# Splitting the row maxima ahead of their transpose in an attention and Fourier-mixing kernel

## The chip, the cores and the metric

The kernel runs on one core of one Trainium2 chip. Its metric is the device time of one execution in microseconds (us). A core has TensorE (PE in the profile; PEld are its weight loads), VectorE (DVE), ScalarE (ACT), GpSimd (POOL) and SyncE (SP), which here only issues DMAs. Each engine takes its instructions in the order in which the program issues them and waits for others through semaphores.

## The reference, cut to what matters

```python
# x: 2048 x 640; 32 heads of 20 columns
g = sigmoid((x * gate_w).sum(-1, keepdims=True))
qkv = (x @ wqkv).reshape(B, S, 3, H, Dh)            # q, k, v per head
scores = einsum("bhqd,bhkd->bhqk", q, k) * Dh ** -0.5
a = einsum("bhqk,bhkd->bhqd", softmax(scores), v)   # -> heads joined, @ wo
b = dft_seq_re @ (x @ dft_hid_re.T) - dft_seq_im @ (x @ dft_hid_im.T)
out = g * a + (1 - g) * b
```

The weights `wqkv` and `wo` are drawn 64 times larger than usual, so scores are large and the softmax needs each row's maximum subtracted before the exponential.

## The kernel before

All is float32. Most matmuls run on numbers rounded to the type fp32r (`R` in the code), each operand split in two rounded parts (`split`: a rounded copy, then the source minus that copy), and three products are added (`three`).

Attention is done by units: a pair of heads and half of the queries (1024), so 32 units (`NU`). Per unit the scores are computed twice. The first time ("m" steps, `s_mm`, line 187) they lie with queries on partitions, and DVE takes the maximum over each 512 keys (line 189) into `mx`. The second time ("e" steps, line 907) they lie with keys on partitions, and ACT takes the exponential (line 909). The negative maximum of each query has to be in the second product already: the query operand `q` has two more rows per head (from row `KROWS`, 60), which hold the two rounded parts of the negative maximum, against rows of ones in the key operand. These rows are filled once per unit:

- `max_nm` (lines 201 to 203): DVE reduces `mx` over the key chunks to `nm`, 128 queries by 16 columns (2 heads, 8 query tiles), negated.
- `max_chain` (lines 218 to 235): TensorE transposes `nm` to 16x128 in a PSUM bank `pt` (line 221; weights are `nm`, the moving operand is the identity), DVE splits it into `m1` and `m2` (lines 114 and 115 through `split`), and two steps later four DMAs on SP's queue copy them to the rows of `q` (lines 229 and 230).

After a first part (projections of q, k, v, the gate), the main part is one loop over 256 cycles. A string of letters in `ORDERS` says in which order TensorE's work is issued in a cycle: "e" and "m" score matmuls, "F" fillers (matmuls of the Fourier part, lines 363 and 608, and of the output projection, line 715), and at the end "B", `burst`:

```python
def burst(c):
    for n in ends:
        max_nm(n)
    run_extras(max(done - HIDS, 0) // 3, 2)
    for kt in (2 * c, 2 * c + 1):
        av_step(now[0], kt // NS, kt % NS)
    while ends:
        max_chain(ends.pop(0))
```

So in every eighth cycle DVE gets `nm` ahead of the 16 matmuls of probabilities by values ("av", line 528), which run in four column tiles of the array, and TensorE gets the transpose behind them. `run_extras` issues the reading of finished Fourier tiles between the two; one of its operations is DVE's addition of line 628. The first unit ends before the loop, where `s_end` calls `max_nm` and, two score steps later, `max_chain`.

The score matmuls and the fillers run in two row tiles of the array (60, 62 or 64 rows). The matmuls of the first part (lines 118 to 120) use the whole array. Five PSUM banks (`bank`) go round among score tiles, transposes and others.

POOL adds and splits the operands of the Fourier part (lines 114, 115, 501, 517, 742). All of its work is from SBUF to SBUF, in instructions of 0.45 to 2.4 us. DVE's work on the maxima reads PSUM, with the exception of `nm`, which reads `mx`.

Of the kernel before, what the change touches and what calls it, by code (L numbers as in the profile page):

```python
# [10 lines left out]
F32 = mybir.dt.float32  # L11
R = mybir.dt.float32r
AF = mybir.ActivationFunctionType
ALU = mybir.AluOpType
AX = mybir.AxisListType
# [3 lines left out]
P = 128  # L19
# [9 lines left out]
KROWS = 3 * DH  # L29
# [41 lines left out]
def f32(ap):  # L71
    return ap.bitcast(F32)
# [3 lines left out]
def mix_kernel(ctx: ExitStack, tc: tile.TileContext, xa, wqk, wb, cdft, wo, out):  # L76
    nc = tc.nc
    pe, act, dve, pool, sp = nc.tensor, nc.scalar, nc.vector, nc.gpsimd, nc.sync
    ctx.enter_context(tc.manual_schedule())

    def pools(**kw):
        return ctx.enter_context(tc.tile_pool(**kw))

    const = pools(name="const", bufs=1)
    small = pools(name="small", bufs=1)
# [14 lines left out]
    ident = const.tile([P, P], F32, name="ident")  # L100
# [9 lines left out]
    def split(dst1, dst2, src, e1, e2):  # L110
        if e1 is act:
            act.activation(dst1, src, AF.Copy)  # L112
        else:
            e1.tensor_copy(dst1, src)  # L114
        e2.tensor_tensor(dst2, src, f32(dst1), op=ALU.subtract)  # L115
# [8 lines left out]
    def bank():  # L124
        return ps_w.tile([P, 512], F32, name=f"ps{next(turn) % 5}")
# [40 lines left out]
    def q_unit(n):  # L166
        p, u = VISITS[n]
        return third["q"] if p == 14 else qst[place(p)][:, u * (S // 2) : (u + 1) * (S // 2)]

    mx, nms, ends = {}, {}, []  # L170
    now, later = [-1], {}

    def at_step(i, fn):
        later.setdefault(i, []).append(fn)
# [16 lines left out]
    def s_end(i):  # L191
        n, s = divmod(i, 32)
        if n < NU and s == 31:
            if now[0] < 0:
                max_nm(n)
            else:
                ends.append(n)
        if s == 1 and 0 < n <= NU and now[0] < 0:
            max_chain(n - 1)

    def max_nm(n):
        nms[n] = small.tile([P, 16], F32, name="nm", bufs=2)
        dve.tensor_reduce(nms[n], mx.pop(n).rearrange("p h q c -> p (h q) c"), axis=AX.X, op=ALU.max, negate=True)

    def s_step(i):
        for fn in [s_mm(i, h) for h in range(2)]:
# [10 lines left out]

    def max_chain(n):
        q = q_unit(n)
        pt = bank()[:16, :P]  # L220
        pe.transpose(pt, nms.pop(n), ident)  # L221
        m1 = small.tile([16, P], R, name="m1")
        m2 = small.tile([16, P], R, name="m2")
        split(m1, m2, pt, dve, dve)

        def rows():
            for h in range(2):
                b = 64 * h + KROWS
                sp.dma_start(f32(q[b : b + 1, :]), f32(m1[8 * h : 8 * h + 8, :]))
                sp.dma_start(f32(q[b + 1 : b + 2, :]), f32(m2[8 * h : 8 * h + 8, :]))  # L230

        if now[0] < 0:
            rows()
        else:
            at_step(now[0] + 2, rows)
# [555 lines left out]
    start = 4 * HID  # L791
# [121 lines left out]
# [8 lines that stand above are left out]
        if c in (HID - NS - 1, HID - 1):  # L921
            next_pool()
# [127 lines left out]
```

## Time and profile before

| | |
|---|---|
| median of 3 runs | 1869.67 us (1867.93 to 1871.03) |
| profiled execution | 1869.47 us |
| its span, first to last instruction | 1867.7 us |
| mean granted TensorE clock | 0.998 |
| DVE `nm`, line 203 | 32 instructions, 210 ns each |
| transpose, line 221: weight load, matmul | 32 each, 87 ns and 277 ns |
| DVE split of `pt`, lines 114 and 115 | 32 each, 278 ns each |

How to read the lines: a timeline line gives the start in us, the duration in us, engine, line, operation, the tile written, an arrow, the tiles read, the shape and a count (instructions merged), and in brackets how long the engine was idle before and what ended that. A line of groups gives the count, busy us and mean ns, and the idle us before. A line of stretches gives the stretch, its length, busy us (and instructions) of PE, PEld, DVE, ACT and POOL, the granted clock, the DMA share and GB/s. The line of a source gives the shortest, median and longest duration in ns. The slices of the page give the busy tenths of an engine in 40 equal parts of the span. Matmul durations include the way through the array, so distances between starts tell more than durations.

### The profile page before, as it was taken

The page shows a single profiled execution, that of the slowest core. Times are in us where ns is not written, and L with a number is a line of the kernel's source. Part 1 is how long each engine was busy: PE and PEld are TensorE (multiplying, and loading weights), DVE is VectorE, ACT ScalarE, POOL GpSimd, SP SyncE. Part 2 cuts the span into 40 slices and gives each one's busy share as a digit, 9 for nine tenths or more (in the row PEclk, how much of TensorE's full clock was granted, in tenths as well). Part 3 has the DMA queues.
Part 4 walks back from the last instruction along what each step waited for, and adds up shares of the span by engine and source line. Part 5 has one row for each costly group of instructions (what it writes and reads, how often), then busy time and mean ns, then how long its engine had stood idle before and what let it go on. Part 6 is the DMA issues. An engine that isn't in the chain of part 4 may idle for free.

```text
span 1867.7 us, 45004 instructions
## 1 busy us (share of the span) xinstructions
PE 1858.3 (100%) x17606; PEld 1360.8 (73%) x17606; DVE 1383.7 (74%) x2310; ACT 1272.1 (68%) x2439; POOL 1162.6 (62%) x1038
## 2 busy tenths in 40 slices
PE   9999999999999999999999999999999999999998
PEld 8988777676767777777777777767777777776666
DVE  3044458787878888888888888888888888888853
ACT  4222258787877777777777777777777777778885
POOL 3335432121146897466799899867779989635544
PEclk9999999999999999999999999999999999999999
DMA  6744341222134674535567576546476766431233
GB/s 230 174 136 151 139 127 56 78 65 68 54 99 139 209 209 142 161 128 175 185 192 241 163 249 191 176 140 179 145 240 203 214 198 202 142 90 47 88 98 108
DMA packets 178771, 281.61 MB, mean 151 GB/s; under 512 B 44811, under 2 KB 113547, under 8 KB 178559
## 3 DMA queue, kind: packets, MB, share of 16 engines
q1 hardware_dynamic: 177599, 276.77, 47.4%
q0 software_dynamic: 960, 1.97, 0.6%
q8 instruction: 138, 2.26, 0.5%
q14 instruction: 74, 0.61, 0.1%
HBM read 214.61 MB, written 63.52 MB: 149 GB/s over the span
## 4 chain that ended last, share of the span: by engine, by line
PE 98%; DMA 1%; POOL 0%; ACT 0%; DVE 0%; issue 0%; SPq 0%; POOLq 0%; ACTq 0%
PE av L528 25%; PE yp L608 19%; PE ps L907 16%; PE ps L187 15%; PE yp L363 7%; PE ps L118 4%; PE ps L120 4%; PE ps L119 4%; PE yp L715 3%; PE ps L221 0%; DMA p<-in_xa 0%; POOL p L115 0%; DMA a_scr<-raw 0%; DVE mx L189 0%; ACT p L323 0%
## 5 line engine op out<-in xcount | busy, mean ns | idle before, releaser
L189 DVE TENSOR_REDUCE mx<-ps 128x1 f32<-128x512 f32 x2048 | 1280.1, 684 | 298.9 <-PE ps L187 280.7
L909 ACT ACTIVATE p<-ps 128x512 f32<-128x512 f32 x2048 | 1109.1, 599 | 371.6 <-PE ps L187 248.9
L187 PE MATMUL ps<-kst,qst 60*128 60x512 f32 x1920 | 758.3, 410 | 0.0
L907 PE MATMUL ps<-qst,kst 62*128 62x512 f32 x1920 | 744.9, 407 | 0.1
L608 PE MATMUL yp<-x,part 64*128 64x320 f32 x5376 | 662.1, 306 | 0.3 <-ACT raw L373 0.3
L608 PEld LDWEIGHTS yp<-x,part 64*128 64x128 f32 x5376 | 624.7, 186 | 8.3 <-ACT raw L373 0.6
L528 PE MATMUL av<-p,v 128*21 128x512 f32 x4096 | 490.1, 596 | 0.0
L907 PEld LDWEIGHTS ps<-qst,kst 62*128 62x128 f32 x1920 | 348.1, 185 | 182.5 <-DVE mx L189 132.2
L187 PEld LDWEIGHTS ps<-kst,qst 60*128 60x128 f32 x1920 | 342.2, 184 | 7.9 <-issue 4.2
L115 POOL TENSOR_TENSOR part<-raw,part 128x1024 fp32r<-128x1024 f32 (+1 forms) x128 | 288.0, 2250 | 10.3
L528 PEld LDWEIGHTS av<-p,v 128*21 128x21 f32 x4096 | 97.6, 100 | 221.5 <-issue 218.3
L363 PE MATMUL yp<-wb,x 64*128 64x320 f32 x1920 | 224.0, 307 | 0.0
L374 POOL TENSOR_TENSOR raw<-raw 128x320 f32<-128x320 f32 x64 | 55.7, 870 | 268.4 <-ACT raw L373 219.1
L363 PEld LDWEIGHTS yp<-wb,x 64*128 64x128 f32 x1920 | 210.1, 186 | 6.0
L114 POOL CAST part<-raw 128x1024 fp32r<-128x1024 f32 (+1 forms) x128 | 126.1, 985 | 127.9 <-PE ps L187 67.0
L501 POOL TENSOR_TENSOR raw<-raw,raw 128x1024 f32<-128x1024 f32 x77 | 185.9, 2414 | 7.5 <-DMA raw<-in_cdft 6.0
L115 POOL TENSOR_TENSOR x<-araw,x 128x320 fp32r<-128x320 f32 x112 | 97.8, 873 | 9.0
L715 PE MATMUL yp<-x,part 64*128 64x320 f32 x768 | 102.2, 308 | 0.0
L323 ACT ACTIVATE p<-ps 128x512 f32<-128x512 f32 x40 | 23.8, 597 | 102.0 <-PE ps L120 85.5
L715 PEld LDWEIGHTS yp<-x,part 64*128 64x128 f32 x768 | 92.0, 186 | 1.0
L118 PE MATMUL ps<-x,part 128*128 128x512 f32 x200 | 80.7, 403 | 1.6 <-ACT x L112 1.3
L114 POOL CAST p<-p 128x512 fp32r<-128x512 f32 x40 | 24.7, 618 | 92.4 <-ACT p L323 92.4
(110 smaller groups left out, 1419.5 us busy)
## 6 DMA issues: line engine op xcount, KB each, us to landing
raw<-in_cdft SPq DMA_DIRECT2D x192, 512.0 KB
araw<-a_scr SPq DMA_DIRECT2D x192, 160.0 KB
qk_scr<-p SPq DMA_DIRECT2D x40, 512.0 KB
kst<-qk_scr SPq DMA_DIRECT2D x84, 160.0 KB
qst<-qk_scr SPq DMA_DIRECT2D x84, 160.0 KB
yt<-y_scr SPq DMA_DIRECT2D x80, 160.0 KB
a_scr<-raw SPq DMA_DIRECT2D x64, 160.0 KB
y_scr<-yt SPq DMA_DIRECT2D x64, 160.0 KB
```

Of the source, the lines that this page charges most:

```text
L114: e1.tensor_copy(dst1, src)
L115: e2.tensor_tensor(dst2, src, f32(dst1), op=ALU.subtract)
L118: pe.matmul(ps, st1, mv1, start=first, stop=False)
L187: pe.matmul(ps, q[b : b + KROWS, qt * P : (qt + 1) * P], k[b : b + KROWS, kc * 512 : (kc + 1) * 512], start=True, stop=True)
L189: return lambda: dve.tensor_reduce(mx[n][:, h, qt, kc : kc + 1], ps, axis=AX.X, op=ALU.max)
L363: pe.matmul(yp[h][:, :HE], x[r, xz, d, cs], w[r, wz, d, :HE], start=d == 0 and z == 0, stop=d == ND - 1 and z == 2)
L501: pool.tensor_tensor(raws[0], raws[0], raws[1], op=ALU.add if PRODUCTS[n][0][1][0] > 0 else ALU.subtract)
L528: pe.matmul(av[32 * j : 32 * j + DH + 1, :], v[:, kt, h * (DH + 1) : (h + 1) * (DH + 1)], pp[qc][:, h, :], start=kt == 0, stop=kt == NS - 1)
L608: pe.matmul(yp[h][:, :HE], c[r, cz, cs], a[r, az], start=s == 0 and z == 0, stop=s == NS - 1 and z == 2)
L715: pe.matmul(yp[h][:, :HE], o[oz][r], wos[d, hf][r, wz], start=d == 0 and z == 0, stop=end)
L907: pe.matmul(pt, k[b : b + KROWS + 2, kt * P : (kt + 1) * P], q[b : b + KROWS + 2, qc * 512 : (qc + 1) * 512], start=True, stop=True)
L909: act.activation(pts[n, kt, qc][:, h], pt, AF.Exp, scale=float(DH) ** -0.5)
```

## The change

The split moves ahead of the transpose. `max_nm` now writes two rounded parts of `nm` side by side into columns 0 to 31 of a tile `turned` (128x128, fp32r, zero beyond, one buffer for all units), with DVE for both steps. In `max_chain` a plain matmul with `turned` as weights and a rounded identity as moving operand gives all 32 rows at once, one DVE copy brings them from PSUM to SBUF, and the four row DMAs read from that copy. Two instructions come in once at the start: a POOL memset of `turned` and a DVE copy of the identity.

```diff
+    turned = small.tile([P, P], R, name="turned")
+    pool.memset(f32(turned), 0.0)
+    ident_r = small.tile([P, P], R, name="ident_r")
+    dve.tensor_copy(ident_r, ident)
+
     def max_nm(n):
-        nms[n] = small.tile([P, 16], F32, name="nm", bufs=2)
-        dve.tensor_reduce(nms[n], mx.pop(n).rearrange("p h q c -> p (h q) c"), axis=AX.X, op=ALU.max, negate=True)
+        nm = small.tile([P, 16], F32, name="nm", bufs=2)
+        dve.tensor_reduce(nm, mx.pop(n).rearrange("p h q c -> p (h q) c"), axis=AX.X, op=ALU.max, negate=True)
+        nms[n] = turned
+        split(nms[n][:, :16], nms[n][:, 16:32], nm, dve, dve)
...
     def max_chain(n):
         q = q_unit(n)
-        pt = bank()[:16, :P]
-        pe.transpose(pt, nms.pop(n), ident)
-        m1 = small.tile([16, P], R, name="m1")
-        m2 = small.tile([16, P], R, name="m2")
-        split(m1, m2, pt, dve, dve)
+        pt = bank()[:, :P]
+        pe.matmul(pt, nms.pop(n), ident_r, start=True, stop=True)
+        mt = small.tile([32, P], F32, name="m1", bufs=2)
+        dve.tensor_copy(mt, pt[:32])
 
         def rows():
             for h in range(2):
-                b = 64 * h + KROWS
-                sp.dma_start(f32(q[b : b + 1, :]), f32(m1[8 * h : 8 * h + 8, :]))
-                sp.dma_start(f32(q[b + 1 : b + 2, :]), f32(m2[8 * h : 8 * h + 8, :]))
+                for z in range(2):
+                    r = 64 * h + KROWS + z
+                    sp.dma_start(f32(q[r : r + 1, :]), mt[16 * z + 8 * h : 16 * z + 8 * h + 8, :])
```

## The prediction

> **What bounds the kernel now.** I read the page's busy times and slices first, then the chain that ended last, then stretches, then the timeline of one turn of the maxima, engine by engine.
>
> ```profile
> PE 1858.3 (100%) x17606; PEld 1360.8 (73%) x17606; DVE 1383.7 (74%) x2310; ACT 1272.1 (68%) x2439; POOL 1162.6 (62%) x1038
> POOL 3335432121146897466799899867779989635544
> PE 98%; DMA 1%; POOL 0%; ACT 0%; DVE 0%; issue 0%; SPq 0%; POOLq 0%; ACTq 0%
> ```
>
> TensorE carries 98% of the chain, so whatever holds it in a turn is lost, and nothing later gives it back. POOL is quiet in the slices in which the first eight units fall and dense in the middle.
>
> ```profile
> 600.00:1660.00 1060.00, 1059.69 (x10760) 761.30 (x10759) 887.81 (x1482) 765.70 (x1420) 850.71 (x679) 1.00 0.58 181
> ```
>
> In this stretch of the table by stretches POOL is busy 850.71 of 1060 us in 679 instructions. Now one turn inside it, the lines of DVE, then the weight loads, then POOL.
>
> ```profile
> 943.51 0.21 DVE L203 TENSOR_REDUCE nm<-mx 128x16 f32<-128x64 f32 x1
> 943.78 0.49 DVE L628 TENSOR_TENSOR m<-yp,m 128x320 f32<-128x320 f32 x1
> 944.58 0.28 DVE L114 CAST m<-ps 16x128 fp32r<-16x128 f32 x1 [0.31 <-PE ps L221]
> 944.89 0.28 DVE L115 TENSOR_TENSOR m<-ps,m 16x128 fp32r<-16x128 f32 x1
> ```
> ```profile
> 944.26 0.09 PEld L221 LDWEIGHTS ps<-ident,nm 128*16 128x16 f32 x1 [0.85 <-DVE m L628]
> 944.47 0.18 PEld L907 LDWEIGHTS ps<-qst,kst 62*128 62x128 f32 x1
> ```
> ```profile
> 943.58 2.37 POOL L115 TENSOR_TENSOR part<-raw,part 128x1024 fp32r<-128x1024 f32 x1
> ```
>
> The reduction `nm` ends at 943.72. The transpose's load starts at 944.26, behind the av burst, and the next load comes 0.21 us later: that 0.21 us is all that a turn costs TensorE. Between `nm` and the load lie 0.54 us. How much of it is free, the first unit shows, whose load follows `nm` at once:
>
> ```profile
> 219.49 0.22 DVE L203 TENSOR_REDUCE nm<-mx 128x16 f32<-128x64 f32 x1
> ```
> ```profile
> 219.76 0.09 PEld L221 LDWEIGHTS ps<-ident,nm 128*16 128x16 f32 x1 [0.67 <-DVE nm L203]
> ```
>
> It takes 0.05 us from the end of `nm` (219.71) to the load. So 0.49 us are free in the later turn, none in the first.
>
> **The matmul instead of the transpose.** It loads 128 columns of weights instead of 16 and streams 128 columns of rounded numbers. No row shows that shape; the nearest are wide rounded matmuls ahead of and behind a change of the array's shape.
>
> ```profile
> 1849.55 0.41 PE L118 MATMUL ps<-x,x 128*128 128x320 f32 x1
> 1849.80 0.31 PE L119 MATMUL ps<-x,x 128*128 128x320 f32 x1
> 1849.94 0.31 PE L120 MATMUL ps<-x,x 128*128 128x320 f32 x1
> ```
> ```profile
> 108.82 0.31 PE L119 MATMUL ps<-wb,x 128*128 128x322 f32 x1
> 108.97 0.30 PE L120 MATMUL ps<-wb,x 128*128 128x322 f32 x1
> 109.20 0.50 PE L187 MATMUL ps<-kst,qst 60*128 60x512 f32 x2
> ```
>
> The first wide matmul after an av burst is followed after 0.25 us, the others after 0.14 to 0.15: its load lies open and costs 0.105. A stream of 320 columns takes 0.147, so 128 take 0.06 in proportion. The change from a full array to row tiles costs 0.23 instead of 0.15, that is 0.085. Sum 0.25 against 0.21 now: +0.05 us (kept from the unrounded parts), in 32 units +1.6 us. The bounds: with the load hidden it is 0.105 less, a gain of 1.8 us in all; if a narrow rounded matmul ran at the pace of the present transpose and more, at most 0.16 more a unit, +5 us.
>
> **The split ahead of it.** Removed behind the transpose is one of two DVE operations of 0.28 us; one copy stays. DVE is not the bound there, so this is worth nothing. Added ahead of the transpose are a copy and a subtraction of 128x16, each behind its forerunner by 0.03 us (944.89 less 944.86).
>
> ```profile
> L442 DVE TENSOR_SCALAR ngate<-gate 128x16 f32<-128x16 f32 x1 | 0.2, 174 | 0.0
> L440 DVE TENSOR_SCALAR gate<-gate 128x16 f32<-128x16 f32 x1 | 0.2, 157 | 0.0
> ```
>
> By these rows of the groups by form they take 0.16 and 0.17, with the gaps 0.40 us. The 0.49 free us cover that with 0.09 to spare; in the first unit they are open, +0.4 us. That is the cost if DVE runs them undisturbed. But these two read SBUF alone, which no DVE instruction of a turn did before, and the timeline of the first stages shows what such an instruction meets beside POOL:
>
> ```profile
> 97.42 1.17 DVE L115 TENSOR_TENSOR wb<-raw,wb 128x966 fp32r<-128x966 f32 x1 [20.23 <-ACT wb L112]
> ```
> ```profile
> 19.23 2.15 DVE L115 TENSOR_TENSOR wb<-raw,wb 128x966 fp32r<-128x966 f32 x1 [2.76 <-ACT wb L112]
> ```
> ```profile
> 19.06 1.30 POOL L115 TENSOR_TENSOR p<-p 128x512 fp32r<-128x512 f32 x1
> ```
> ```profile
> 135.99 0.82 DVE L115 TENSOR_TENSOR part<-raw,part 128x640 fp32r<-128x640 f32 x1 [3.04 <-ACT part L112]
> ```
> ```profile
> 136.09 1.88 POOL L115 TENSOR_TENSOR p<-p 128x512 fp32r<-128x512 f32 x1
> ```
>
> The same subtraction of two SBUF tensors takes 1.17 us alone and 2.15 where a POOL instruction was already running: 2.15 less 1.17 puts its real start at 20.21, 0.15 before POOL's recorded end (20.36). The other way round POOL takes 1.88 instead of 1.30 where DVE came first, and is let in 0.14 before DVE's end (136.81). So one holds the other off for its whole instruction, and whoever waits gets in next. The new subtraction is of that kind. For the copy the nearest rows disagree:
>
> ```profile
> L550 DVE RECIPROCAL lc<-lc x31: 240/243/247, 328.3 to 1812.6; 128x16 f32<-128x16 f32 x31
> ```
> ```profile
> L1000 DVE COPY rb<-lc 128x512 f32<-128x512 f32 x1 | 0.4, 426 | 0.0
> ```
>
> A one-input reciprocal is never held (240 to 247 ns in all 31). But above the 0.16 us of a 16-element operation a copy takes 0.27 us for 496 more elements, the subtraction 1.01 for 950: half as much an element. So the copy moves two at a time, and I infer that it uses the second path that the two-input subtraction uses. I take the copy as held too. The Trainium skill, page "SBUF — State Buffer", section "Who interferes with whom", says so: copies in a two-port mode and operations with two SBUF inputs share a port pair with GpSimd, locked for a whole instruction. By it the sum is the one below; its part on copies no run here shows.
>
> How long they wait, by POOL's groups in the stretch 600 to 1660:
>
> ```profile
> L115 POOL TENSOR_TENSOR part<-raw,part 128x1024 fp32r<-128x1024 f32 x110 | 262.6, 2388 | 8.8
> L501 POOL TENSOR_TENSOR raw<-raw,raw 128x1024 f32<-128x1024 f32 x77 | 185.9, 2414 | 7.5 <-DMA raw<-in_cdft 6.0 <-PE ps L187 1.5
> L114 POOL CAST part<-raw 128x1024 fp32r<-128x1024 f32 x110 | 114.2, 1038 | 127.7 <-PE ps L187 67.0 <-PE yp L608 46.4 <-PE ps L907 10.6
> L115 POOL TENSOR_TENSOR x<-araw,x 128x320 fp32r<-128x320 f32 x96 | 83.8, 873 | 7.7
> L517 POOL TENSOR_TENSOR araw<-araw 128x320 f32<-128x320 f32 x80 | 69.9, 874 | 0.7 <-DMA araw<-a_scr 0.7
> ```
>
> At a random moment the rest of a running instruction is the sum of count times duration squared, over twice the stretch: 627 + 449 + 119 + 73 + 61 us², and about 70 for the smaller groups, over 2120, is 0.66 us; less the 0.14 of tail in 80% of moments, 0.55. That holds the copy. In the meantime POOL's next instruction has come up and goes in behind it, and the subtraction waits for all of that: 850.71/679 less 0.14 is 1.11 us, where one was met (0.80) and the next is queued (only the 110 casts of `part`, one in six, come after long idle: 0.84), 0.75. Less the 0.09 to spare in 80% of cases, a unit waits 1.23 us. The row of `nm` at 943.51 is such a case: POOL's 2.37 us started 0.17 before the copy would.
>
> ```profile
> L203 DVE TENSOR_REDUCE nm<-mx x21: 207/210/212, 640.4 to 1650.5; 128x16 f32<-128x64 f32 x21
> ```
>
> 21 units lie in the stretch: 26 us. For the ten others besides the first, most of them in quiet slices of POOL, I take 1.5 us together, an estimate by the slices.
>
> **What queues behind.** Behind the held pair on DVE stand `m` of line 628 (0.49 us, in some turns) and the copy of the result; TensorE waits with its whole in-order queue, the e and m score matmuls first. The four row DMAs on SP are the same four, two steps later as now. The setup (a POOL memset, a DVE copy of the identity) lies ahead of the first loaded data and costs nothing I can see; at most its own 0.5 us.
>
> **The clock.** Waits of 2 us have a second price. Before the steady part, one table row has TensorE busy 1.93 of 3.41 us, and in the next 3.41 us the granted clock is 0.50:
>
> ```profile
> 7.39:10.80 3.41, 1.93 (x7) 1.03 (x7) 1.71 (x3) 2.26 (x5) 0.00 (x0) 1.00 1.00 377
> 10.80:14.21 3.41, 3.41 (x10) 2.64 (x9) 2.91 (x5) 2.78 (x4) 0.00 (x0) 0.50 0.35 111
> ```
>
> So 1.48 idle us within such a window cost half of the next, 1.7 us. A unit that meets one of the 2.4-us instructions (448 of 1060 us, 0.42) waits 1.1 + 0.9 = 2.0 on average and by my estimate passes 1.48 in two of three cases: 21 x 0.42 x 0.67 = 6 units, of which some four or five put it in one window: 8 us. The Trainium skill, page "TensorE: Matmul & The Clock Gate", section "The HAM clock gate", asks for a whole idle window of about 3.4 us before the clock halves. By it these 8 us would not come; the row above, with TensorE 57% busy, speaks against it.
>
> **The sum**, against the profiled execution's 1869.47 us (span 1867.7; the median of the runs, 1869.67, is 0.2 above): 1.6 + 0.4 + 26 + 1.5 + 8 = 37.5, so 1907 us.
>
> **The rivals.** What a measurement of this kernel can tell from no change is about 0.2%, 3.7 us.
> - The clock stays full: the waits come, their second price doesn't: 29.5, so 1899 us. For it: the row shows it once, in the cold start. 0.20.
> - Only the subtraction is held. Then a unit waits 0.55 less 0.07, 21 x 0.48 = 10 us; with 0.4, 1.6, 0.5 and one or two slow windows (3) 15.5, so 1885 us; without those 1882. For it: the reciprocal's constant time. 0.15.
> - Nothing is held: 128x16 is short enough to slip in, or POOL yields. Then the 0.49 free us hide the split, and only 1.6 + 0.4 stay: 1871.5 us, no change that can be told. Decided at 0.09 us of wait a unit: below it, this case. Against it: 2.15 instead of 1.17. 0.10.
> - TensorE's step gets cheaper by more than I bound, with nothing held: load hidden, it gains 1.8, 1867.7; past 3.7 it would have to lose the change of shape too. 0.02.
>
> My forecast has 0.53; in it a narrow matmul at 0.16 more a unit would only add 5 us. Slower by over 0.2%: 0.53 + 0.20 + 0.15 = 0.88; within: 0.10; faster: 0.02. The range reaches from the third case without slow windows, 1882, to 1930: waits of 1.8 us a unit (38) and ten slow windows (17) with the 3.5 of the rest give 1928. It leaves out the last two cases and a little above.
>
> **What would show it.** Per unit, in the changed profile: the copy and the subtraction on DVE with means far above 0.16 and 0.17 us in the middle of the span and at them elsewhere, each starting inside a POOL instruction; the load of `turned` waiting for the subtraction; 0.25 us from that load to the next; stretches at a clock of 0.50 just after the longest waits. I am wrong if the copy and the subtraction stay near 0.16 and 0.17 us beside POOL (then nothing is held), or if the waits come and later turns are shorter for them.

## The result and the profile after

The changed kernel is slower: 1902.05 us median (1900.62 to 1904.07, 6 runs) against 1870.65 us for the kernel before (1867.93 to 1871.2, 6 runs), a ratio of 1.0171 with a 95% interval of 1.0157 to 1.0184. That is 31.4 us more. The profiled execution took 1900.62 us, its span is 1898.5 (1867.7 before).

The page first: busy times, POOL's slices, and the shares of the chain that ended last.

```profile
PE 1863.9 (98%) x17606; PEld 1367.3 (72%) x17606; DVE 1419.5 (75%) x2343; ACT 1271.8 (67%) x2439; POOL 1163.1 (61%) x1039
POOL 4335422121146896566799799767779979635544
PE 91%; DVE 7%; DMA 1%; POOL 0%; ACT 0%; issue 0%; SPq 0%; POOLq 0%; ACTq 0%; DVEq 0%
```

POOL's busy time is that of before (1163.1 us against 1162.6), and TensorE has as many instructions; TensorE's share of the chain fell from 98% to 91%, and what came in its place is DVE. Now the same turn that the prediction showed at 943.51, the fifteenth unit (952.74 here): DVE, then the weight loads, then POOL.

```profile
952.74 0.21 DVE L208 TENSOR_REDUCE nm<-mx 128x16 f32<-128x64 f32 x1
952.98 2.22 DVE L114 CAST turned<-nm 128x16 fp32r<-128x16 f32 x1
955.23 0.17 DVE L115 TENSOR_TENSOR turned<-nm,turned 128x16 fp32r<-128x16 f32 x1
955.33 0.48 DVE L634 TENSOR_TENSOR m<-yp,m 128x320 f32<-128x320 f32 x1
```
```profile
955.46 0.19 PEld L228 LDWEIGHTS ps<-ident_r,turned 128*128 128x128 f32 x1 [2.82 <-DVE turned L115]
955.72 0.18 PEld L913 LDWEIGHTS ps<-qst,kst 62*128 62x128 f32 x1
```
```profile
952.82 2.35 POOL L115 TENSOR_TENSOR part<-raw,part 128x1024 fp32r<-128x1024 f32 x1
955.89 0.88 POOL L748 TENSOR_TENSOR yt<-yt,m 128x320 f32<-128x320 f32 x1 [0.72 <-DVE m L634]
```

The reduction ends at 952.95. POOL's subtraction had begun 0.16 us before the copy, and the copy, 0.17 us of work where nothing meets it, is recorded as 2.22: it ends at 955.20, just after POOL's 955.17. The subtraction of `turned` then runs freely, for POOL's next instruction wasn't ready: it waited for `m` of line 634, which DVE has queued behind the split. TensorE's load waited 2.82 us, against 0.85 in the turn shown before. Where POOL does have its next instruction ready, the subtraction pays, as in the unit at 1160 (DVE, then POOL):

```profile
1160.31 0.48 DVE L114 CAST turned<-nm 128x16 fp32r<-128x16 f32 x1
1160.83 2.26 DVE L115 TENSOR_TENSOR turned<-nm,turned 128x16 fp32r<-128x16 f32 x1
```
```profile
1159.90 0.87 POOL L115 TENSOR_TENSOR x<-araw,x 128x320 fp32r<-128x320 f32 x1
1160.72 2.34 POOL L507 TENSOR_TENSOR raw<-raw,raw 128x1024 f32<-128x1024 f32 x1
```

Summed up by the groups of instructions by form, over all 32 units (count, busy us and mean ns, idle us of the engine before them), first the load before the change, then the same load and the split after it:

```profile
L221 PEld LDWEIGHTS ps<-ident,nm 128*16 128x16 f32 x32 | 2.8, 87 | 26.9 <-DVE nm L203 20.2 <-DVE m L628 5.9 <-DVE yt L731 0.8
```
```profile
L228 PEld LDWEIGHTS ps<-ident_r,turned 128*128 128x128 f32 x32 | 6.0, 186 | 52.7 <-DVE turned L115 50.6 <-issue 1.2 <-DVE yt L737 0.8
L114 DVE CAST turned<-nm 128x16 fp32r<-128x16 f32 x32 | 22.1, 689 | 1.2
L115 DVE TENSOR_TENSOR turned<-nm,turned 128x16 fp32r<-128x16 f32 x32 | 15.9, 497 | 1.1
```

The loads of weights stood idle for 52.7 us ahead of the turn instead of 26.9: 25.8 of the 30.8 us by which the span grew.

### The profile page after: what moved, and what is told of

Read it like the earlier page. It is cut to its first block, busy times and chain, and to the rows that moved or that the text cites. A ratio compares the mean times of both kernels' runs of the same rounds, so it can differ in the third digit from the quotient of the medians.

```text
span 1898.5 us, 44988 instructions
## 1 busy us (share of the span) xinstructions
PE 1863.9 (98%) x17606; PEld 1367.3 (72%) x17606; DVE 1419.5 (75%) x2343; ACT 1271.8 (67%) x2439; POOL 1163.1 (61%) x1039
## 3 DMA queue, kind: packets, MB, share of 16 engines
q8 instruction: 138, 2.26, 0.5%
## 4 chain that ended last, share of the span: by engine, by line
PE 91%; DVE 7%; DMA 1%; POOL 0%; ACT 0%; issue 0%; SPq 0%; POOLq 0%; ACTq 0%; DVEq 0%
PE av L534 23%; PE yp L614 17%; PE ps L913 15%; PE ps L187 14%; PE yp L369 7%; DVE mx L189 5%; PE ps L118 4%; PE ps L119 4%; PE ps L120 4%; PE yp L721 3%; DVE turned L114 1%; DVE turned L115 1%; PE ps L228 0%; DMA p<-in_xa 0%; POOL p L115 0%; DMA a_scr<-raw 0%
## 5 line engine op out<-in xcount | busy, mean ns | idle before, releaser
L114 POOL CAST p<-p 128x512 fp32r<-128x512 f32 x40 | 24.7, 618 | 89.6 <-ACT p L329 89.6
```

## The experiments

Times are medians. The kernel before, run beside them, had 1869.56 us (13 runs) in the first four, 1869.66 (21 runs) in the next four (`pool_in_halves`, `split_early`, `nm_in_psum_5`, `two_row_tiles`), and 1869.61 (21 runs) in the last pair. A ratio, given with its 95% interval, is taken over all runs and need not equal that of the two medians. "After" is the changed kernel, and diffs are against it unless said otherwise.

**Which of the two is held, and does it hang on where they read?** Three kernels take DVE's SBUF reads away one at a time. A reduction can write PSUM, and it can write the rounded type.

`nm_in_psum`: the copy reads PSUM alone, and the subtraction reads one operand from PSUM and one from SBUF.

```diff
-        nm = small.tile([P, 16], F32, name="nm", bufs=2)
+        pb = bank()                    # max_chain's result uses columns 0 to 127 of it
+        nm = pb[:, P : P + 16]
...
```

> The changed kernel with one thing moved: the reduced maxima nm lie in spare columns of the result's PSUM bank, so the copy reads PSUM alone and the subtraction one PSUM and one SBUF tensor. Order, number of instructions, wide matmul and result copy are as in the changed kernel. Theory (DVE is held because its operands lie in SBUF beside POOL): copy and subtraction take 0.16 to 0.18 us in every unit, no long wait of TensorE, 1872 to 1874 us (about 1.6 for the wide matmul and 0.5 for the first unit over before). Rival 1 (the longer chain ahead of the matmul is the price, wherever the operands lie): 1902 us. Rival 2 (the wide matmul itself): 1902 us too.

`sub_held_only`: the first rounded part comes from a second reduction instead of the copy, so only the subtraction is left that can be held.

```diff
...                     # raw is mx, as max_nm reads it
-        split(nms[n][:, :16], nms[n][:, 16:32], nm, dve, dve)
+        dve.tensor_reduce(turned[:, :16], raw, axis=AX.X, op=ALU.max, negate=True)
+        dve.tensor_tensor(turned[:, 16:32], nm, f32(turned[:, :16]), op=ALU.subtract)
```

> The first rounded part comes straight from a second reduction over mx, so no DVE copy from SBUF is left; the subtraction still reads two SBUF tensors. Theory: the subtraction now meets the running POOL instruction first, as the copy did (in the changed kernel that cost 0.70 us a unit in the stretch of 21 units); 13 to 15 us of waits, one or two half-clock windows, 1885 to 1892 us. If only copies were held: 1872 to 1874. If the order and length of the chain were the price: 1902.

`copy_held_only`: `nm` is reduced twice, to PSUM and to SBUF; the copy reads the SBUF one, the subtraction the PSUM one.

```diff
...                     # pb = bank(), raw as above
+        for t in (pb[:, P : P + 16], nm):
+            dve.tensor_reduce(t, raw, axis=AX.X, op=ALU.max, negate=True)
+        dve.tensor_copy(turned[:, :16], nm)
+        dve.tensor_tensor(turned[:, 16:32], pb[:, P : P + 16], f32(turned[:, :16]), op=ALU.subtract)
```

> The maxima are reduced twice, into PSUM and into SBUF. The copy reads the SBUF one, the subtraction the PSUM one, so the copy alone can be held by POOL. Theory (a copy from SBUF is held too): copies of up to 2.2 us in the middle of the span, subtractions of 0.16 to 0.18 everywhere; 14 us of waits, 2 to 3 us because the second reduction uses up the spare time, two half-clock windows; 1887 to 1894 us. If only two-input operations are held: 1874 to 1876 us.

Measured: 1869.86 us (ratio 1.0001, 0.9992 to 1.0011), 1888.49 (1.0099, 1.008 to 1.0119) and 1894.22 (1.0123, 1.0103 to 1.0142). In the groups by form, the copy and subtraction of the first, the pair of the second, and that of the third:

```profile
L114 DVE CAST turned<-ps 128x16 fp32r<-128x16 f32 x32 | 5.6, 175 | 1.2
L115 DVE TENSOR_TENSOR turned<-ps,turned 128x16 fp32r<-128x16 f32 x32 | 5.6, 174 | 1.1
```
```profile
L212 DVE TENSOR_TENSOR turned<-nm,turned 128x16 fp32r<-128x16 f32 x32 | 22.7, 708 | 1.1
L211 DVE TENSOR_REDUCE turned<-mx 128x16 fp32r<-128x64 f32 x32 | 6.7, 209 | 0.0
```
```profile
L212 DVE CAST turned<-nm 128x16 fp32r<-128x16 f32 x32 | 21.8, 680 | 1.2
L213 DVE TENSOR_TENSOR turned<-ps,turned 128x16 fp32r<-128x16 f32 x32 | 5.6, 174 | 1.1
```

The same instruction of 0.17 us has a mean of 0.68 to 0.71 when all that it reads lies in SBUF, and of 0.17 when the copy's source, or one operand of the subtraction, lies in PSUM. Each of the two is held for itself, the copy too, which the prediction had only inferred. In us over the kernel before: neither +0.3, subtraction alone +18.9, copy alone +24.7, both +31.4. These are not pure prices of one hold: the third kernel reduces twice, and in it, as in `nm_in_psum`, the first unit takes 3.3 us longer (below). Both held cost less than the sum of the two; I read that as one POOL instruction that holds whichever comes first, and is over for the other. The second kernel falls into its expected range, the third 0.2 us above it. `nm_in_psum`, at 1869.86, lies 2 us below the range of its expectation, which names the wide matmul and the first unit; to that I return below.

**What if nobody waits for the split?** `split_unawaited` is the kernel before, with the same two instructions written to a tile that nothing reads.

```diff
+    spare = small.tile([P, 32], R, name="spare")
     def max_nm(n):
...
+        split(spare[:, :16], spare[:, 16:32], nms[n], dve, dve)
```

> The kernel before, with the same copy and subtraction of nm into a spare tile that nobody reads, at the place where the changed kernel has them; the transpose waits for nm alone. Theory: the two are held as in the changed kernel (means near 0.7 and 0.5 us), but TensorE meets it only through DVE's lateness behind them (maxima that free PSUM banks late); a third to a half of the price stays, 1876 to 1884 us. Rival (the price is only that the matmul's weights wait for the split): 1870.5 to 1872 us.

Measured: 1888.38 us (1.0101, 1.0086 to 1.0116), above what was expected. The transpose no longer waits, but DVE's queue does, and TensorE runs into it a little later. The waits of the weight loads (total, times, longest), and one such case, DVE, POOL and TensorE:

```profile
PEld yp L611 <- DVE m L631: 9.6, 6, 2.5
PEld ps L910 <- DVE m L115: 8.1, 7, 2.0
```
```profile
1055.13 2.30 DVE L115 TENSOR_TENSOR spare<-nm,spare 128x16 fp32r<-128x16 f32 x1
1057.66 0.28 DVE L115 TENSOR_TENSOR m<-ps,m 16x128 fp32r<-16x128 f32 x1
```
```profile
1055.02 2.38 POOL L504 TENSOR_TENSOR raw<-raw,raw 128x1024 f32<-128x1024 f32 x1
```
```profile
1057.99 0.50 PE L910 MATMUL ps<-qst,kst 62*128 62x512 f32 x1 [1.73 <-DVE m L115]
```

The held subtraction delays DVE's split of the transpose's bank, and the score matmul that needs a free bank waits 1.73 us. The kernel before has no such line; these two hold 17.7 us, some of it beside matmuls that still ran, where the whole loss is 18.8. So a held DVE costs three fifths as much as the change (18.8 of 31.4 us) even where no matmul waits for the split.

**Shorter POOL instructions.** `pool_in_halves` is after, with POOL's addition, copy and subtraction of 1024 columns in two of 512 each.

```diff
+            for k in range(2):
+                cs = slice(512 * k, 512 * (k + 1))
...                     # pool.tensor_tensor and split on [:, cs] instead of the whole
```

> The changed kernel, with POOL's 1024-wide work on the Fourier coefficients (add, cast, subtract; 2.4, 1.04 and 2.4 us) issued as two halves of 512 each. Theory (DVE is held until the POOL instruction that is running ends): no copy or subtraction waits over about 1.3 us, the waits of TensorE add up to two thirds of the 25 us, none long enough for a half-clock window unless both are held; 1885 to 1892 us. If POOL held DVE by its work and not by the instruction: 1902 us or more, since POOL's work grows by some per cent.

Measured: 1886.7 us (1.0092, 1.0078 to 1.0106): nearly half of the loss is gone with POOL doing the same work, as the first theory had it. No stretch of its loop ran at half clock, where after has three. The groups by form again, but of the middle 21 units alone, after and then the halves:

```profile
L114 DVE CAST turned<-nm 128x16 fp32r<-128x16 f32 x21 | 18.3, 871 | 0.7
L115 DVE TENSOR_TENSOR turned<-nm,turned 128x16 fp32r<-128x16 f32 x21 | 12.8, 611 | 0.7
L228 PEld LDWEIGHTS ps<-ident_r,turned 128*128 128x128 f32 x21 | 3.9, 186 | 40.6 <-DVE turned L115 40.6
```
```profile
L114 DVE CAST turned<-nm 128x16 fp32r<-128x16 f32 x21 | 9.6, 455 | 0.7
L115 DVE TENSOR_TENSOR turned<-nm,turned 128x16 fp32r<-128x16 f32 x21 | 12.7, 605 | 0.7
L228 PEld LDWEIGHTS ps<-ident_r,turned 128*128 128x128 f32 x21 | 3.9, 186 | 31.5 <-DVE turned L115 31.5
```

The copy's wait fell from 0.70 to 0.28 us a unit. The subtraction's stayed at 0.43 (0.44 before the halving). I read this as the second half or the next instruction being ready more often, so that what is won in length is lost in how often one is met; that part is only argued.

**The split earlier.** `split_early` calls `max_nm` at once in `s_end`, in the middle of a cycle, so that it should be done long before the turn.

```diff
         if n < NU and s == 31:
-            if now[0] < 0:
-                max_nm(n)
-            else:
+            max_nm(n)
+            if now[0] >= 0:
                 ends.append(n)
```

> The changed kernel, with nm and its split issued to DVE right behind the unit's last first-pass score (in the middle of a cycle) instead of at the cycle's end, so 2 to 3 us more lie between the split and the matmul that needs it. Theory: the matmul no longer waits, but a held DVE frees no PSUM banks, as in the run with the unawaited split, where TensorE stopped about 1 us after DVE; waits of over 1 us are still paid in part; 1876 to 1888 us. Rival (only the matmul's wait for its weights costs): 1870 to 1873 us.

Measured: 1929.45 us (1.032, 1.03 to 1.034), far above. The waits of the weight loads, and one of them on DVE and TensorE:

```profile
PEld ps L187 <- DVE mx L189: 40.1, 25, 3.3
```
```profile
1114.51 2.27 DVE L115 TENSOR_TENSOR turned<-nm,turned 128x16 fp32r<-128x16 f32 x1
```
```profile
1114.06 0.30 PE L613 MATMUL yp<-x,part 64*128 64x320 f32 x1
1117.43 0.79 PE L187 MATMUL ps<-kst,qst 60*128 60x512 f32 x1 [3.06 <-DVE mx L189]
```

My expectation thought of the turn alone. In mid-cycle DVE takes one maximum of 0.68 us after another out of the five banks; any hold there is a score bank that isn't freed, and TensorE stops behind it. Ahead of the av burst, where the change has it, DVE's delay at least lies beside 16 matmuls that need none of these banks. Even the seven units that fall in POOL's quiet slices paid: the cycle ahead of the turn took 6.68 us against 6.16, about DVE's undisturbed 0.57 us of reduction, copy and subtraction. These waits and the seven windows at half clock (1.7 us each) make 52 of the 54.4 us by which the profiled span is longer than before's; by the medians the kernel is 59.8 us slower.

**The wide matmul.** `nm_in_psum_5` repeats the first kernel with more runs. `two_row_tiles` changes it so that the array keeps its two row tiles: two matmuls of 64 rows and 64 columns, into two banks, each with its own copy.

```diff
-        pe.matmul(pt, turned, ident_r, start=True, stop=True)
+        for h in range(2):
+            r = slice(64 * h, 64 * h + 64)
+            pe.matmul(pts2[h], turned[r], ident_r[r, r], start=True, stop=True)
```

> The run with nm in PSUM again, in five rounds beside its neighbours. Its wide matmul step takes 0.256 us against 0.206 of the transpose, and the first unit's 0.4 us are open, so 1.5 to 2.5 us above before; if the result copy in one piece instead of two gives something back, 0 to 1 us.

> As the run with nm in PSUM, with the turning matmul as two matmuls in the two row tiles of the array (64 queries each, 64 columns of the identity), into two banks with two result copies of 32x64. The step then has the array shape of the score matmuls behind it. Theory (of the 0.256 us of the step 0.085 are the change of shape behind it and 0.03 the longer stream): the next score's load comes 0.11 to 0.15 us after the step's first load, 1866 to 1868.5 us. Rival (the change of shape from the av burst is paid anyway and nothing else is saved): 1869 to 1871 us.

Measured: 1870.62 us (1.0007, 0.9998 to 1.0016) and 1869.96 (1.0008, 0.9999 to 1.0016). The repetition, 1.0 us above the kernel before, falls into the second case of its expectation; that the copy in one piece is the reason isn't shown. I take the length of a cycle with a turn from the starts of the av matmuls in the trace, median over a stage. In the middle stage it is 6.49 us before, 6.52 with the wide matmul and 6.37 with the two row tiles, whose step takes 0.11 us from its first load to the next score's, as the theory had it. The whole time is the rival's all the same. In the quiet stage the row tiles make the cycle 6.50 instead of 6.37, and the first unit, which has no cover, now waits for its two matmuls in turn. The weight loads of these two, and the stretches there (busy us of PE, PEld, DVE, ACT, POOL, then the granted clock, the DMA share and GB/s):

```profile
220.54 0.18 PEld L232 LDWEIGHTS ps<-ident_r,turned 64*128 64x128 f32 x1 [0.70 <-issue]
222.98 0.28 PEld L232 LDWEIGHTS ps<-ident_r,turned 64*128 64x128 f32 x1 [2.26 <-DVE m L235]
```
```profile
218.89:222.30 3.41, 1.52 (x15) 1.05 (x12) 3.16 (x9) 0.00 (x0) 0.47 (x1) 1.00 0.00 0
222.30:229.12 6.82, 6.13 (x21) 4.78 (x22) 2.13 (x5) 0.77 (x2) 0.87 (x1) 0.50 0.24 90
```

The gain of 23 turns goes into one wait and its half clock, and into seven quiet turns.

`nm_in_psum` and its repetition pay in the first unit too, and far more than the 0.4 to 0.5 us that their expectations name. There `nm` takes one of the five banks, the four score matmuls up to the turn take the others, and the next score matmul needs the first bank again, so it waits for the copy of the result. Its load in `nm_in_psum`:

```profile
221.72 0.19 PEld L187 LDWEIGHTS ps<-kst,qst 60*128 60x128 f32 x2 [1.67 <-DVE m L232]
```

A window at half clock follows (from 222.38). From the first `nm` to the first av matmul it takes 43.64 us in `nm_in_psum`, 45.51 with the two row tiles and 40.32 in the kernel before. From the first av matmul to the last the order is the other way round: 1601.51, 1599.93 and 1602.14.

Two last kernels change the first unit and the quiet turns. `two_rows_late` keeps the first unit's `nm` in SBUF and issues its turn four score matmuls later (`s == 3` instead of `s == 1` in `s_end`); `two_rows_late_8` also turns units 0 to 7 by the one wide matmul.

```diff
-        if s == 1 and 0 < n <= NU and now[0] < 0:
+        if s == 3 and 0 < n <= NU and now[0] < 0:
...                     # two_rows_late_8 alone:
+        if n < 8:
+            pe.matmul(pb[:, :P], turned, ident_r, start=True, stop=True)
```

> The kernel of the two row tiles, but the first unit (whose maxima are complete ahead of the loop) keeps its maxima in SBUF, has no cover to lose by it, and its matmuls come four score matmuls later, so that TensorE needn't wait for the split there and the slow clock behind that wait goes. Theory (what the two row tiles lost were the first unit's wait with 3 to 4 us at half clock, and 0.13 us in each of the seven quiet turns; their 0.11 us in each later turn is a true gain): about 0.11 x 23 - 0.13 x 7 + 0.6 = 2.2 us under the kernel before, 1867 to 1868. Rival (the 0.11 us of a turn are given back in the cycles behind it): within 0.7 us of the kernel before, 1869 to 1870.5.

> As the run before, and the seven quiet units behind the first turn both parts by one matmul over the full array, the later ones by two row tiles. Theory: the quiet turns then cost 0.05 us more than before's instead of 0.13, so about 0.11 x 23 - 0.05 x 7 + 0.6 = 2.8 us under the kernel before, 1866 to 1867.5. Rival (given back in the cycles behind): 1869 to 1870.5.

Measured: 1873.38 us (1.0015, 1.0007 to 1.0024) and 1868.39 (0.9994, 0.9985 to 1.0003). The slow clock at the first unit is gone in both. The turn in the middle stage takes 6.42 and 6.41 us in them, so of the 0.11 us that the theory counts for a turn 0.07 to 0.08 are left. Both missed: the first lies above both of its ranges, the second between them.

The second is 1.2 us under the kernel before, which its interval doesn't tell from no change; so no version of this idea is shown to beat the kernel before. Why the first is slower stays open. Its profiled span, 1868.3, is short among its 11 runs, whose median is 1870.3 (the kernel before has 1867.8). From the first av matmul to the last this trace took 1604.56 us, 2.4 more than before: its turns are shorter, but its cycles without a turn have a mean of 6.315 us in the middle stage, against 6.296.

## Why the prediction was right

It forecast 1907 us, a range of 1882 to 1930 and slower with a chance of 0.88; 1902.05 was measured, and the mechanism is the one forecast. The profiled execution was to take 37.5 us more than 1869.47 and took 31.2. Step by step:

- **Covered and open turns.** As predicted, an undisturbed split is free. The shortest copy and subtraction of the 32 take 174 ns each, as the source's line shows, and in such turns behind an av burst the load comes after the same 0.85 us of idle as before.

```profile
L114 DVE CAST turned<-nm x32: 174/238/2216, 218.2 to 1826.3; 128x16 fp32r<-128x16 f32 x32
L115 DVE TENSOR_TENSOR turned<-nm,turned x32: 174/176/2262, 218.4 to 1827.1; 128x16 fp32r<-128x16 f32 x32
```

- **The copy is held.** This was inferred against the reciprocal's constant time. `copy_held_only` shows it: 680 ns against 175. The Trainium skill, page "SBUF — State Buffer", section "Who interferes with whom", says that copies can enter a two-port mode and then share a pair of ports with GpSimd, while reductions never do; 175, 680 and, for the reduction beside them, 209 ns agree with this, though no run here shows the ports themselves.
- **The 21 units: 26 us predicted, 22.8 measured** (40.6 us of idle ahead of the loads, by the row above, less the 17.8 before).

```profile
L221 PEld LDWEIGHTS ps<-ident,nm 128*16 128x16 f32 x21 | 1.8, 87 | 17.8 <-DVE nm L203 11.9 <-DVE m L628 5.9
```

  The total hides two misses that go against each other. The copy waited 871 - 174 = 0.70 us a unit, not 0.55: six of the 21 met a 2.4-us instruction near its start and waited over 1.6 us, where random moments give 187 x (2.26 - 1.6)/1060, or 2.4 of 21. Whether that is chance or the two engines' rhythm stays open. The subtraction waited 611 - 174 = 0.44 us, not 0.75. The step "POOL's next instruction has come up and goes in behind it" failed: 16 of 21 copies met an instruction (the 0.80 assumed is 17), but only eight of the subtractions behind them did. Of the other eight, POOL waited in three for `m` of line 634, which DVE has queued behind the split (as at 955.89); in two it had nothing to start for longer; and in three its next instruction began within 0.01 us of the subtraction and did not hold it.
- **The other units:** 25.8 - 22.8 = 3.0 us measured, 1.5 + 0.4 predicted. The first unit lost 0.55; one quiet unit (588.77) met a long subtraction of POOL after all and lost 1.26; two late ones lost 0.6 each.
- **The wide matmul:** 0.25 us from load to load was worked out, 0.26 is measured (955.46 to 955.72), in all 32 units. Yet `nm_in_psum`, where nothing is held, lies only 0.3 us above the kernel before, and its second measurement 1.0, although its first unit alone takes 3.3 us longer. Its cycles without a turn took 6.265 us in the middle stage, against 6.286 before; what shortens them I don't know. In after they took 6.289, so there nothing of the kind sets off the wide matmul.
- **The clock:** four or five windows were predicted, 8 us; three came, at 697.86, 1267.89 and 1629.70, 3 x 1.7 = 5.1. The step that failed is the threshold of 1.48 us idle, taken from a cold start: seven windows of the loop had more than that, and the four with 1.49 to 1.60 us idle were not followed by half clock. Stretches of after, each with the one behind it:

```profile
694.45:697.86 3.41, 1.32 (x13) 0.78 (x10) 2.78 (x4) 0.05 (x1) 3.27 (x4) 1.00 0.00 0
697.86:701.27 3.41, 3.41 (x27) 3.41 (x25) 2.28 (x4) 2.33 (x4) 2.84 (x2) 0.50 0.04 10
...
953.86:957.27 3.41, 1.81 (x18) 1.72 (x20) 3.18 (x6) 0.96 (x2) 2.69 (x3) 1.00 0.02 5
957.27:960.68 3.41, 3.41 (x43) 2.85 (x43) 3.39 (x7) 3.00 (x7) 3.12 (x6) 1.00 0.16 34
...
1264.48:1267.89 3.41, 1.67 (x17) 1.31 (x15) 3.18 (x5) 0.54 (x2) 2.69 (x3) 1.00 0.00 0
1267.89:1271.30 3.41, 3.41 (x26) 3.41 (x24) 2.17 (x4) 2.19 (x5) 3.27 (x5) 0.50 0.03 7
```

  Busy for 1.32 and 1.67 of 3.41 us, TensorE lost half of the next window; at 1.81, which is 1.60 idle, it didn't.

Together 25.8 + 1.6 + 5.1 = 32.5, where the span grew by 30.8. The difference lies ahead of the first turn, where nothing is held yet:

```profile
217.85 0.22 DVE L208 TENSOR_REDUCE nm<-mx 128x16 f32<-128x64 f32 x1
```

The first `nm` starts 1.64 us earlier than the 219.49 of the trace before, which had the window at 0.50 in its cold start (10.80:14.21) that the prediction shows; after's trace has none there. This start differs from trace to trace, 216.75 to 221.25 us in the twelve, so spans of single traces can't be compared to 1 or 2 us. From the first av matmul to the last, after took 1634.11 us and the kernel before 1602.14: 32.0 us more. The rivals fall by rows of their own: "only the subtraction" by the copy's 689 ns, "nothing is held" by both means (689 and 497 ns), the cheaper TensorE step by its 0.26 us. "The clock stays full" gave 1899 us, which is nearer to the 1902 measured than my 1907; by the time alone it would stand, and only the three windows at 0.50 decide against it.

## What to carry to other kernels

Before small SBUF-to-SBUF work of DVE is put ahead of something that TensorE needs, look at what GpSimd runs at that place: the price isn't the instruction's 0.17 us but the rest of GpSimd's, here up to 2.1 us, and everything in DVE's queue pays it even if nobody waits for the result. Letting the producer write PSUM, so that the consumer reads PSUM, took that price away at the cost of no instruction; but it takes a PSUM bank earlier, and in the first unit TensorE waited 1.67 us for that bank. And the free time that covers a step belongs to a place in the schedule, not to the step: half a cycle earlier the same split cost nearly twice as much.

## What the runs showed of the hardware

- TensorE's clock halves for a window of 3.41 us without a wholly idle one before it. The Trainium skill, page "TensorE: Matmul & The Clock Gate", section "The HAM clock gate", describes windows of 3413 ns that run on regardless of the kernel; the trace agrees, since from 697.86 to 1267.89 and on to 1629.70 are 167.0 and 106.0 of them. The page puts the idle state after an idle window; here one with 1.67 us of work was enough. The border isn't one number of busy time, though: in `split_unawaited` a window with 1.75 us of work was followed by half clock, in `copy_held_only` one with 1.52 was not. The first two lines are of the former, the last two of the latter.

```profile
694.86:698.27 3.41, 1.75 (x19) 1.14 (x15) 3.34 (x5) 1.08 (x2) 3.27 (x4) 1.00 0.02 5
698.27:701.68 3.41, 3.41 (x22) 3.41 (x24) 2.48 (x4) 1.59 (x3) 3.17 (x2) 0.50 0.02 5
```
```profile
1108.46:1111.87 3.41, 1.52 (x17) 0.29 (x9) 3.34 (x7) 0.86 (x3) 2.97 (x2) 1.00 0.00 0
1111.87:1115.28 3.41, 3.41 (x37) 3.32 (x39) 3.20 (x7) 2.60 (x5) 2.99 (x4) 1.00 0.02 4
```
- A turn by two matmuls of 64 rows, which keep the array's two row tiles, makes the cycle 0.10 to 0.15 us shorter than one matmul over the full array in the middle stage (6.42, 6.41 and 6.37 in three kernels, against 6.52 us), and 0.07 to 0.08 us longer in the quiet one (6.49 and 6.50 against 6.42). What turns the sign is open.
